# Four more chunks of q and k turned by a copy in DRAM and VectorE instead of by TensorE

## The chip, the cores and the metric

The kernel runs on one core of one Trainium2 chip. Five engines run their own instruction queues and meet at semaphores: TensorE (in the profile PE for matmuls, PEld for weight loads), VectorE (DVE), ScalarE (ACT), GpSimd (POOL) and SyncE (SP), which here does nothing but issue DMAs. A core has 16 DMA engines. The metric is the device time of one execution in microseconds; lower is better.

## The reference

Two blocks follow each other. The first is a linear attention with decay ("lightning attention"): batch 4, 8 heads, 768 positions, head dimension 64, in blocks of 64 positions.

```
for b in range(nb):                       # blocks of 64 positions
    intra = einsum(qb, kb) * Dmask        # lower triangular, lam ** distance
    out   = einsum(intra, vb) + einsum(qb * lam_pow, kv_state)
    kv_state = lam_block * kv_state + einsum(kb * rev_pow, vb)
```

The second takes the result as x, 3072 rows (batch times position) of 512, and runs four dense experts, each weighted by its share of the domain probabilities:

```
p = domain_probs / domain_probs.sum(-1)
for e in range(4):                        # w1[e]: 512 x 1024, w2[e]: 1024 x 512
    out += p[:, e:e+1] * (relu(x @ w1[e]) @ w2[e])
```

All is float32. The experts' products are the bulk of the arithmetic.

## The kernel before

**Tiling.** The 3072 rows are cut into three groups of 1024 (`NG` = 3), and each group with each of the four experts is a unit: 12 units, numbered 0 to 11 in the order of `units`. The products of a unit are made by Strassen's scheme with seven products, in most places nested twice, so that sums of blocks of the weights and of x are made by POOL, VectorE and through DRAM (`w1_ops`, `w2_ops`, `w2_sums`, `x_blocks`). While unit `at` makes its second product (line 1204, `w2t`), the first product of the next unit is made beside it (line 1145, weights in `ws_in`). Both go through seven products `i`, and each `i` through eight slots `x`. The order of all work is written out by this loop: slot number (`at` * 7 + `i`) * 8 + `x`. Outside of attention a product takes 12.95 us, so a slot is about 1.6 us. Unit 0 starts at 88.4 us of the trace, unit 1 at 191.4, unit 2 at 293.8. From unit 5 (`NEST`) on, other forms of the products take over.

**Attention** works on chunks of 128 positions of one batch: 6 chunks times 4 batches, n = 0 to 23, eight to a group. `where(n)` gives (chunk, batch). The first eight are made ahead of unit 0. The other 16 stand in the slots named by `AT`, from n = 8 on: slot `AT[n - 8]` is where `scores(n)` is issued, together with `values(n - 1)`. n = 8 to 15 are chunks 2 and 3, with (2,0), (2,1), (3,0), (3,1), (2,2), (2,3), (3,2), (3,3) in this order, n = 16 to 23 chunks 4 and 5 likewise. For each, `attention()` puts steps into the slots: `load_more(n)` (q and k), `load(n, "v")` seven slots ahead of the scores, `turn(n)`, and the scores.

**Turning.** Scores need q and k with the head dimension on the partitions. Two ways are there:

- By TensorE (`turn`, line 698): q and k are loaded as they lie (two DMAs each), eight transposes of 128x128 go to the PSUM banks s0 and s1, and ACT copies the two results to SBUF (lines 706 and 707). Before the change this is so for n = 0 to 15. Loads stand 7 slots ahead of the turn, and the turn 4 ahead of the scores; for n = 12 (`TURNED_FIRST`) these are 5 and 7.
- Across (`turn_across`, line 678), before the change for n = 16 to 23 (`comes_across`): DMAs from DRAM to DRAM first copy q and k into `across`, in stripes of 32 columns, so that 32 of the head dimension's columns of each head stand as rows of blocks of 32x32. `load_across` reads four blocks a head and partition (runs of 512 B), and VectorE transposes every 32x32 block of the 128x512 tile in place, one instruction for q and one for k. k is loaded once more as it lies, for the state's update (`decayed`, on POOL). Loads stand 5 slots ahead of the turn, and the turn 7 ahead of the scores.

**The copies** are 128 DMAs (`pieces`): for each batch 16 of q and then 16 of k, each of 32 columns of one head over chunks 4 and 5, in runs of 128 B, 256 runs in all. `trickle` issues the next one: one a step in the products that lead up to unit 0, one a slot in unit 0 (in odd slots from ACT's queue, else from SyncE's), and from unit 1 on one in every odd slot. Ahead of the loads of a chunk, `load_more` issues at once what is still missing of its batch.

**Order around the change.** SyncE issues its DMAs strictly in the program's order, and waits where one has to wait. On it stand, from slot to slot: the weights of the second product (`feed2`, three products ahead), those of the first (`feed`, in unit 1 in slots 0 and 1 of a product for the product after it), stores of sums made by POOL, the copies, and the loads of q, k and v. Work on VectorE that is not bound to a slot waits in the lists `lately` (attention) and `background` (operands of the experts) and is taken about one a slot, `lately` first. A planner's estimates (`busy`, `moved`, `asked`, `filled`) decide when POOL's chores begin.

Of the kernel before, what the change touches and what calls it, by code (L numbers as in the profile page):

```python
# [14 lines left out]
FP32 = mybir.dt.float32  # L15
# [6 lines left out]
def kernel(  # L22
# [32 lines left out]
    B, H, S, D = q.shape  # L55
    E, DM, F = moe_w1.shape
    NTOK, DOUT = out.shape
    P = nc.NUM_PARTITIONS
    C = P
    BL = C // 2  # L60
    NHP = H // 2
    NCH = S // C
    CPG = 8
    G = CPG * C
    NG = NTOK // G
# [14 lines left out]
    dram = ctx.enter_context(tc.tile_pool(name="sums", bufs=1, space=DRAM))  # L80
# [11 lines left out]
    def small(name):  # L92
        return pool.tile([P, W], FP32, name=name, tag="t")
# [7 lines left out]
    def packet(ap):  # L101
        n, step = 1, 1
        for stride, size in reversed(ap.ap[1:]):
            if stride != step or size == 1 and stride != 1:
                break
            n, step = n * size, step * size
        return n

    def send(out, in_, by=None):
        n = 4 * min(packet(out), packet(in_))  # L110
        moved[0] = max(moved[0], now[0]) + 4 * math.prod(out.shape) / n * (9 + n / 25) / 16 / 1714
        if by is None:
            asked[0] = max(asked[0], now[0]) + 0.27
        (by or nc.sync).dma_start(out=out, in_=in_)
# [35 lines left out]
    def where(n):  # L150
        g, x = divmod(n, CPG)
        return (x // 4, x % 4) if g == 0 else (2 * g + x // 2 % 2, 2 * (x // 4) + x % 2)
# [304 lines left out]

    SECOND = NCH - 2  # L460
    across = dram.tile([2, P, NHP, B, 8, 32], FP32, name="across")
    pieces = []

    def bring_across(b):
        for x, of in enumerate((q, k)):
            for y in range(4):
                for ac in range(NHP):
                    src = of[b, 4 * (y // 2) + ac, SECOND * C:, (y % 2) * 32:(y % 2 + 1) * 32]
                    to = across[x, y * 32:(y + 1) * 32, ac, b]
                    pieces.append((b, lambda by, to=to, src=src: send(  # L470
                        out=to, in_=src.rearrange("(t p) d -> p t d", p=32), by=by,
                    )))

    def trickle(m=1, by=None):
        for _ in range(m):
            if pieces:
                pieces.pop(0)[1](by)

    def comes_across(n):
        return where(n)[0] >= SECOND  # L480

    def load_across(n):
        c, b = where(n)
        for x, name in enumerate("qk"):
            t = small(f"{name}x")
            send(
                out=t[:].rearrange("p (h c) -> p h c", c=C),
                in_=across[x, :, :, b, (c - SECOND) * 4:(c - SECOND) * 4 + 4].rearrange("p h t d -> p h (t d)"),
            )
            nat[n, name + "x"] = t  # L490

    def load_more(n):
        if not comes_across(n):
            load(n, "qk")
        else:
            trickle(sum(b <= where(n)[1] for b, _ in pieces))
            load_across(n)
            load(n, "k")

# [38 lines left out]
    for r in range(2):  # L538
        for ac in range(NHP):
            h = 4 * r + ac  # L540
# [102 lines left out]
    def rest(n=1, force=False):  # L643
        for _ in range(n):
            take(background, force)
# [9 lines left out]
    def decayed(n):  # L655

        kn = nat[n, "k"]
        kd = kn if n >= CPG else small("kd")[:].rearrange("p (h d) -> p h d", d=D)
        nat[n, "kd"] = kd
        by = k_decay.rearrange("p r ac -> p ac r").unsqueeze(3).to_broadcast([P, NHP, 2, D])  # L660
        tt(nc.gpsimd, *(x.rearrange("p (ac r) d -> p ac r d", r=2) for x in (kd, kn)), by, ALU.mult)
# [194 lines left out]
        ))  # L856

    FILL = {1: 18, 2: 43}
    AT = (34, 40, 47, 53, 58, 94, 101, 108, 115, 147, 154, 167, 172, 203, 210, 223)
    TURNED_FIRST = CPG + 4  # L860
    steps = []

    def attention():

        first, last = CPG, NG * CPG - 1
        for n in range(first, last + 1):
            s = AT[n - first]
            turns_at = s - (7 if comes_across(n) or n == TURNED_FIRST else 4)

            def both(n=n):  # L870
                if n > first:
                    values(n - 1, ("s0", "s1"))
                scores(n, ("q02", "q12"))

            steps.append((turns_at - (5 if comes_across(n) or n == TURNED_FIRST else 7), lambda n=n: load_more(n)))
            steps.append((s - 7, lambda n=n: load(n, "v")))
            steps.append((turns_at, lambda n=n: turn(n, ("s0", "s1"))))
            if comes_across(n):
                steps.append((turns_at, lambda n=n: (decayed(n), nat.pop((n, "k")))))
            steps.append((s, both))  # L880
        steps.append((AT[last - first] + 5, lambda: values(last, ("s0", "s1"))))
        steps.append((AT[last - first] - 14, turn_gates))
        steps.sort(key=lambda s: s[0])
# [711 lines left out]
    def put_back():  # L1595
        n = len(copied)
        while copied:
            copied.pop(0)()
        return n
# [162 lines left out]
        lambda: own_weights("M1"), sum_own("S1", "A21", "A22", ALU.add), *w2_steps[0:4], mine["M1"], *w2_steps[4:],  # L1762
        raw["A12"],
    ))
    for b in range(B):
        bring_across(b)
    for m in SEQ0[2:]:
        if m == SEQ0[-1]:
# [42 lines left out]
    for at, (g, e) in enumerate(units):  # L1811
# [14 lines left out]
        for i in range(7):  # L1826
# [12 lines left out]
            if nested:  # L1839
                pair = (at * 7 + i) % 2 if ahead else i % 3  # L1840
                idle[:] = [(("q11", "q12"), ("q01", "q02"))[pair % 2], False]
                b = nested_product(at, SEQ3[i], (("q01", "q02"), ("q11", "q12"), ("g1", "g3"))[pair])
                if i < 6 and (at, SEQ3[i + 1]) != PLAIN:
                    inner_sums(at, SEQ3[i + 1])
            else:
                b = second_product(g, e, SEQ2[i], banks)
# [21 lines left out]
            for x, part in enumerate(order):  # L1868
                for f in part:
                    if f:  # L1870
                        f()
                now[0] += 1
                put = False
                if at == 0:
                    idle[:] = [("s0", "s1"), i < 3]
                    put = put_back()
                    take(own_sums)
                if nested and ahead:
                    idle[1] = x in (1, 4) and (at - 2 * E + 1, i, x) not in held_at
                    put = put_back()  # L1880
                added = first_steps.pop((at - 2 * E + 1, i, x), None)
                if added:
                    added()
                all_added(now[0])
                if joins and not background:
                    joined()
                elif added and x > 2 or put:
                    pass
                elif (ahead or x % 2 == 0 and x + i) and not (nests and i == 6 and x == 7):
                    if nested or nests:  # L1890
                        if lately:
                            take(lately)
                        else:
                            rest()
                        if at == 2 * E and i in (2, 3) and fits():
                            rest()
                    else:
                        took = False
                        for of in (lately, background, own_sums):
                            if of and (not took or fits() or of is background and len(of) > 4):  # L1900
                                take(of)
                                if of is lately and i == 0:
                                    take(of)
                                took = True
                if nested or nests:
                    take(aside)
                    if own_sums and (nested or fits()):
                        take(own_sums)
                if ending and fits():
                    end_first()  # L1910
                if nested and ahead and x in (1, 3) and fill3:
                    feed3(*fill3.pop(0))
                if turned_back and x > 0:
                    for y in turned_back.pop(0):
                        if SEQ3[i] == END[1]:
                            give(*y[:2], ("s0", "s1"), *y[2:])
                        else:
                            give_across(*y)
                if fill and at * 7 + i >= 6 and x in ((0, 1) if at * 7 + i < 13 else (1, 3, 5) if at * 7 + i == 13 else FEED[nested]):
                    feed(*fill.pop(0))  # L1920
                while steps and (at * 7 + i) * 8 + x == steps[0][0]:
                    steps.pop(0)[1]()
                if at == 0 or x % 2:
                    trickle(1, nc.scalar if at == 0 and x % 2 else None)
                for h in range(1, NG):
                    if x == 3 and 0 <= at * 7 + i - FILL[h] < 7:
                        x_fill(h, SEQ[at * 7 + i - FILL[h]])
                pump(PACE[g])
# [30 lines left out]
```

## Time and profile before

| | |
|---|---|
| median of 3 executions | 1144.79 us (1144.61 to 1146.84) |
| the profiled execution | 1146.52 us |
| its span, first to last instruction | 1144.7 us |
| TensorE busy (matmuls) | 1135.0 us, 99% of the span |
| VectorE, ACT, POOL busy | 765.6, 384.1, 766.5 us |
| moved by DMA | 269.22 MB, mean 235 GB/s |
| chain that ended last | PE 95%, POOL 2%, DVE 1%, issue 1% |

The page's first part gives busy times; its second cuts the span into 40 slices (28.6 us each) with a digit for the busy share in tenths, 9 being 90% or more. A group's line gives the source line, the engine, the operation, what is written from what is read, shapes and count, then busy time and mean ns of one, then the engine's idle time before it and what ended it. In the order of time, a line gives start and length in us. Landing times of DMAs are from issue to the last byte's semaphore.

### The profile page before, as it was taken

How to read it: one execution, taken by the hardware profiler on the slowest of the kernel's cores; microseconds unless marked ns; L12 is line 12 of the kernel's file. 1: busy time of each engine (PE TensorE's matmuls, PEld its weight loads, DVE VectorE, ACT ScalarE, POOL GpSimd, SP SyncE). 2: the span in 40 equal slices, each digit the busy share in tenths (PEclk: the TensorE clock that was granted, in tenths of full speed). 3: DMA queues.
4: the chain of work that ended last, by engine and by line, in shares of the span. 5: the costliest groups of instructions: out<-in, count | busy, mean ns of one | idle time of the engine just before them, and what ended most of it. 6: DMA issues, size and time to landing. Idle time of an engine off the chain costs nothing.

```text
span 1144.7 us, 22214 instructions
## 1 busy us (share of the span) xinstructions
PE 1135.0 (99%) x8015; PEld 990.5 (87%) x8015; DVE 765.6 (67%) x1466; ACT 384.1 (34%) x776; POOL 766.5 (67%) x734
## 2 busy tenths in 40 slices
PE   9999999999999999999999999999999999999998
PEld 7788888888888888888888888888888888888887
DVE  5576676576577748837665566778757576776785
ACT  4325223213312321232343442444354442342332
POOL 2657148646852974853884997895995783873885
PEclk9999999999999999999999999999999999999999
DMA  9795788898999999977867658976678757657552
GB/s 201 166 276 174 196 222 248 271 301 231 307 315 298 296 314 290 309 271 241 250 207 255 197 182 286 331 247 210 204 252 262 230 158 195 202 163 210 173 193 74
DMA packets 309148, 269.22 MB, mean 235 GB/s; under 512 B 141424, under 2 KB 244016, under 8 KB 309040
## 3 DMA queue, kind: packets, MB, share of 16 engines
q1 hardware_dynamic: 291360, 262.66, 75.2%
q10 hardware_dynamic: 17648, 5.15, 2.1%
q8 instruction: 64, 1.05, 0.4%
q14 instruction: 44, 0.36, 0.1%
q0 software_dynamic: 32, 0.00, 0.0%
HBM read 194.83 MB, written 77.10 MB: 238 GB/s over the span
## 4 chain that ended last, share of the span: by engine, by line
PE 95%; POOL 2%; DVE 1%; issue 1%; DMA 0%; ACT 0%; DVEq 0%; POOLq 0%; ACTq 0%
PE pg L1145 39%; PE pq L1511 23%; PE q L1204 21%; PE pM L1653 2%; PE pc L1653 2%; PE op L795 1%; PE sp L732 1%; PE op L813 1%; PE sp L739 1%; POOL acc L117 1%; PE qp L698 1%; PE pM L1378 1%; PE kp L698 1%; PE pg L1511 1%; DVE m L117 0%
## 5 line engine op out<-in xcount | busy, mean ns | idle before, releaser
L1145 PE MATMUL pg<-xs,ws_in 128*128 128x256 f32 x1960 | 470.7, 380 | 0.5 <-DVE m L117 0.5
L1145 PEld LDWEIGHTS pg<-xs,ws_in 128*128 128x128 f32 x1960 | 370.5, 190 | 54.4 <-DVE m L117 4.0
L117 DVE TENSOR_TENSOR m<-pg,m 128x512 f32<-128x512 f32 x374 | 255.9, 686 | 97.0 <-PE pg L1145 84.6
L1204 PE MATMUL q<-w2t,m 128*128 128x256 f32 x1120 | 265.5, 380 | 0.0
L1204 PEld LDWEIGHTS q<-w2t,m 128*128 128x128 f32 x1120 | 211.7, 190 | 29.2 <-issue 0.3
L117 DVE TENSOR_TENSOR sums<-pq,sums 128x256 f32<-128x256 f32 x272 | 113.2, 421 | 90.4 <-PE pq L1511 78.4
L117 POOL TENSOR_TENSOR m<-m,decay 128x512 f32<-128x512 f32 x91 | 114.7, 1273 | 81.5 <-ACT m L1162 64.6
L1511 PE MATMUL pq<-acc,w2t 128*128 128x256 f32 x688 | 169.2, 379 | 0.0
L1511 PEld LDWEIGHTS pq<-acc,w2t 128*128 128x128 f32 x688 | 130.5, 190 | 18.0
L1162 ACT ACTIVATE m<-m 128x512 f32<-128x512 f32 x99 | 62.4, 630 | 195.4 <-DVE m L117 190.5
L1222 DVE SCALAR_TENSOR_TENSOR acc<-q,gate,acc 128x256 f32<-128x256 f32 x108 | 52.1, 482 | 79.2 <-PE q L1204 78.7
L117 DVE TENSOR_TENSOR m<-m,m 128x512 f32<-128x512 f32 x108 | 91.1, 843 | 6.5 <-ACT m L1128 6.5
L1158 ACT COPY m<-pg 128x512 f32<-128x512 f32 x88 | 51.6, 586 | 122.6 <-PE pg L1145 118.5
L117 POOL TENSOR_TENSOR acc<-hT,hT 128x512 f32<-128x512 f32 x56 | 70.4, 1273 | 22.3 <-DVE hT L117 12.1
L1122 ACT COPY pg<-m 128x512 f32<-128x512 f32 x77 | 45.4, 590 | 111.0 <-DVE m L117 103.9
L117 POOL TENSOR_TENSOR acc<-hT,acc 128x512 f32<-128x512 f32 x56 | 71.3, 1273 | 6.5 <-PE pq L1511 2.7
L1511 PE MATMUL pq<-hT,w2t 128*128 128x256 f32 x288 | 70.0, 379 | 0.0
L117 POOL TENSOR_TENSOR w2o<-w2b 128x512 f32<-128x512 f32 x26 | 34.9, 1364 | 44.9 <-DMA w2b<-in_moe_w_dram 27.4
L1511 PEld LDWEIGHTS pq<-hT,w2t 128*128 128x128 f32 x288 | 54.7, 190 | 7.4
L117 POOL TENSOR_TENSOR kn<-kn,decay 128x512 f32<-128x512 f32 x16 | 18.5, 1157 | 59.8 <-PE kp L698 35.5
L1511 PE MATMUL pq<-m,w2t 128*128 128x256 f32 x228 | 55.4, 379 | 0.0
L1126 ACT COPY m<-pg 128x512 f32<-128x512 f32 x44 | 25.8, 586 | 88.2 <-PE pg L1145 83.5
(157 smaller groups left out, 1463.6 us busy)
## 6 DMA issues: line engine op xcount, KB each, us to landing
w2t<-w_ops SPq DMA_DIRECT2D x129, 256.0 KB, 3.2
ws_in<-w_ops SPq DMA_DIRECT2D x40, 512.0 KB, 4.4
ws_in<-w_ops SPq DMA_DIRECT2D x60, 256.0 KB, 3.9
ws_in<-w_ops SPq DMA_DIRECT2D x40, 384.0 KB, 4.1
w2b<-in_moe_w_dram SPq DMA_DIRECT2D x56, 256.0 KB, 5.4
w_ops<-ops SPq DMA_DIRECT2D x28, 512.0 KB, 4.8
w2t<-w_sums SPq DMA_DIRECT2D x40, 256.0 KB, 4.3
w_sums<-w2o SPq DMA_DIRECT2D x16, 512.0 KB, 4.1
```

The costliest lines, as they stand in the source:

```text
L117: eng.tensor_tensor(out=o, in0=a, in1=b, op=op)
L698: nc.tensor.transpose(out=x[:, ac * C:(ac + 1) * C], in_=y[:, 2 * ac:2 * ac + 2].rearrange("p r d -> p (r d)"), identity=ident[:],)
L732: nc.tensor.matmul(out=sp[r][half[x], ac * BL:(ac + 1) * BL], lhsT=hc(kT)[half[r], ac, blk[x]], rhs=hc(qT)[half[r], ac, blk[x]], start=(ac ...
L1122: nc.scalar.copy(out=banks[tags[1]][:], in_=new["11"][:])
L1126: nc.scalar.copy(out=o[:], in_=p[:])
L1145: nc.tensor.matmul(out=p[:, j * 256:(j + 1) * 256], lhsT=ws[i][:, j * P:(j + 1) * P], rhs=xs[i], start=(fresh and j == 0), stop=True, skip ...
L1158: nc.scalar.copy(out=new[at][:], in_=p[:])
L1162: nc.scalar.activation(out=new[at][:], in_=new[at][:], func=AF.Relu)
L1204: nc.tensor.matmul(out=p[:, s * DH:(s + 1) * DH], lhsT=h[A_OF[m]][:, c * 256 + s * P:c * 256 + (s + 1) * P], rhs=fed2[g, e, m][uu][:, c], ...
L1222: nc.vector.scalar_tensor_tensor(out=o, in0=x, scalar=w, in1=o, op0=ALU.mult, op1=ALU.add)
L1511: nc.tensor.matmul(out=p[:, 0:256], lhsT=fed3[e, m, x // 2][:, x % 2, c * P:(c + 1) * P], rhs=b[B_OF[i]][:, c * 256:(c + 1) * 256], start= ...
L1653: nc.tensor.matmul(out=p[:, s * 256:(s + 1) * 256], lhsT=a[c][:, f:f + P], rhs=b[:, c, j * 256:(j + 1) * 256], start=(s == 0 and c == 0 an ...
```

## The change

- `comes_across(n)` is now n >= 12 (`FIRST_ACROSS` = `CPG` + 4), so that n = 12 to 15, chunks 2 and 3 of batches 2 and 3, go across as well. TensorE's 32 transposes and ACT's 8 copies for them go, 8 transposes on VectorE come.
- The tile `across` has 16 blocks of 32 positions in place of 8, from chunk 2 on. The copies of batches 2 and 3 take all four chunks 2 to 5 (512 runs of 128 B, 64 KB), those of batches 0 and 1 chunks 4 and 5 as before (256 runs, 32 KB). There are still 128 copies.
- Their order is by `rank`: batch 0 (short), 2 (long), 3 (long), 1 (short), where it was 0, 1, 2, 3.
- In unit 1 one more copy goes out in each product, in slot 4.
- Scores of n = 13 and 14 move from slots 94 and 101 to 91 and 99. With the loads 12 slots ahead of the scores, chunk n = 12 is loaded in slot 46 as before, n = 13 in slot 79 (before 83), n = 14 in 87 (before 90), n = 15 in 96 (before 97).
- `TURNED_FIRST` goes, since n = 12 has its distances by `comes_across`.

```diff
-    SECOND = NCH - 2
-    across = dram.tile([2, P, NHP, B, 8, 32], FP32, name="across")
+    FIRST_ACROSS = CPG + 4
+    across = dram.tile([2, P, NHP, B, 16, 32], FP32, name="across")
     pieces = []
+    rank = {0: 0, 2: 1, 3: 2, 1: 3}

     def bring_across(b):
+        c = min(where(n)[0] for n in range(FIRST_ACROSS, NG * CPG) if where(n)[1] == b)
         for x, of in enumerate((q, k)):
             for y in range(4):
                 for ac in range(NHP):
-                    src = of[b, 4 * (y // 2) + ac, SECOND * C:, (y % 2) * 32:(y % 2 + 1) * 32]
-                    to = across[x, y * 32:(y + 1) * 32, ac, b]
-                    pieces.append((b, lambda by, to=to, src=src: send(
+                    src = of[b, 4 * (y // 2) + ac, c * C:, (y % 2) * 32:(y % 2 + 1) * 32]
+                    to = across[x, y * 32:(y + 1) * 32, ac, b, (c - 2) * 4:]
+                    pieces.append((rank[b], lambda by, to=to, src=src: send(
                         out=to, in_=src.rearrange("(t p) d -> p t d", p=32), by=by,
                     )))
...
     def comes_across(n):
-        return where(n)[0] >= SECOND
+        return n >= FIRST_ACROSS
...
-                in_=across[x, :, :, b, (c - SECOND) * 4:(c - SECOND) * 4 + 4].rearrange("p h t d -> p h (t d)"),
+                in_=across[x, :, :, b, (c - 2) * 4:(c - 1) * 4].rearrange("p h t d -> p h (t d)"),
...
-            trickle(sum(b <= where(n)[1] for b, _ in pieces))
+            trickle(sum(x <= rank[where(n)[1]] for x, _ in pieces))
...
-    AT = (34, 40, 47, 53, 58, 94, 101, 108, 115, 147, 154, 167, 172, 203, 210, 223)
-    TURNED_FIRST = CPG + 4
+    AT = (34, 40, 47, 53, 58, 91, 99, 108, 115, 147, 154, 167, 172, 203, 210, 223)
...
-            turns_at = s - (7 if comes_across(n) or n == TURNED_FIRST else 4)
+            turns_at = s - (7 if comes_across(n) else 4)
...
-            steps.append((turns_at - (5 if comes_across(n) or n == TURNED_FIRST else 7), lambda n=n: load_more(n)))
+            steps.append((turns_at - (5 if comes_across(n) else 7), lambda n=n: load_more(n)))
...
-    for b in range(B):
+    for b in rank:
         bring_across(b)
...
-                if at == 0 or x % 2:
+                if at == 0 or x % 2 or at == 1 and x == 4:
                     trickle(1, nc.scalar if at == 0 and x % 2 else None)
```

## The prediction

> **What bounds the kernel now.** I read the page's first two parts, then stretches of the time in which the four chunks are loaded, then the groups by line, then TensorE's and SyncE's instructions in order of time there. From the page:
>
> ```profile
> span 1144.7 us, 22214 instructions
> PE 1135.0 (99%) x8015; PEld 990.5 (87%) x8015; DVE 765.6 (67%) x1466; ACT 384.1 (34%) x776; POOL 766.5 (67%) x734
> ...
> PEclk9999999999999999999999999999999999999999
> DMA  9795788898999999977867658976678757657552
> ```
>
> TensorE is the bound, at full clock, and nothing but its work counts. The view of stretches (engines' busy time, then clock, share of the 16 DMA engines, GB/s) shows the next resource behind it:
>
> ```profile
> 88.40:191.40 103.00, 103.00 (x910) 90.52 (x909) 70.25 (x143) 33.22 (x68) 57.23 (x61) 1.00 0.73 200
> 191.40:219.70 28.30, 28.30 (x249) 24.57 (x248) 12.81 (x31) 8.34 (x17) 21.81 (x27) 1.00 0.80 260
> 219.70:261.70 42.00, 42.00 (x318) 36.93 (x318) 29.63 (x48) 7.06 (x15) 18.39 (x19) 1.00 0.99 304
> ```
>
> TensorE has no idle time in any of them, and from 219.7 to 261.7 us the DMA engines have none either (0.99). The groups by line give what is removed and what replaces it (busy, mean of one):
>
> ```profile
> L698 PE MATMUL qp<-ident,qn 128*128 128x128 f32 x64 | 10.5, 288 | 0.0
> L698 PE MATMUL kp<-ident,kn 128*128 128x128 f32 x64 | 10.1, 283 | 0.1
> L706 ACT COPY qT<-qp 128x512 f32<-128x512 f32 x16 | 9.4, 590 | 31.5 <-PE qp L698 31.5
> L678 DVE STREAM_TRANSPOSE qx<-qx 128x512 f32<-128x512 f32 x8 | 5.6, 698 | 0.0
> ```
>
> TensorE's instructions in order of time around chunk 13's turn:
>
> ```profile
> 249.08 1.89 PE L1204 MATMUL q<-w2t,m 128*128 128x256 f32 x8
> 250.81 0.60 PE L698 MATMUL qp<-ident,qn 128*128 128x128 f32 x4
> 251.24 0.60 PE L698 MATMUL kp<-ident,kn 128*128 128x128 f32 x4
> 251.68 1.89 PE L1145 MATMUL pg<-xs,ws_in 128*128 128x256 f32 x8
> ```
>
> The transposes start at 250.81 and the next product at 251.68: a turn holds TensorE 0.87 us. SyncE's queue in order of time (start, time to issue), around the loads of chunks 13 and 14:
>
> ```profile
> 231.65 0.57 SPq L114 DMA_DIRECT2D across<-in_k_dram  x1
> ...
> 233.38 0.42 SPq L114 DMA_DIRECT2D ws_in<-w_ops  x1
> ...
> 237.83 1.09 SPq L174 DMA_DIRECT2D qn<-in_q_dram  x2
> ...
> 248.36 0.46 SPq L114 DMA_DIRECT2D ws_in<-w_ops  x1
> ...
> 252.29 0.42 SPq L114 DMA_DIRECT2D ws_in<-w_ops  x1
> ...
> 257.14 4.52 SPq L174 DMA_DIRECT2D kn<-in_k_dram  x2
> ```
>
> Call the three ws_in feeds X, Y and Z: X and Y bring the first parts of the weights for products 4 and 5 of unit 1, Z the second part for product 5. They landed 5.7, 6.0 and 10.1 us after issue, so at 239.1, 254.4 and 262.4. TensorE's first matmuls with them started at 247.35, 263.40 and 268.6. Margins: 8.2, 9.0 and 6.2 us. That 10.1, and two kn issues of 4.52 us, show a queue that is already full.
>
> **The change, part by part.**
>
> Removed from TensorE: 4 chunks x 8 transposes, 4 x 0.87 = **3.5 us**. TensorE has no idle time from 88 us on beyond a few tenths here and there, so without a new wait all of it comes off the end (a 0.6 us wait for POOL and VectorE at 741.8 could take some back).
>
> Removed from ACT: 8 copies of 0.59 us; added on DVE: 8 transposes of 0.70 us, 5.6 us in all. DVE is busy 70.25 of 103.00, 12.81 of 28.30 and 29.63 of 42.00 us in the stretches concerned, which hides them; without that cover they cost 5.6 us. Among the eight chunks that already go this way, one whose transpose stands a slot ahead of its scores made TensorE wait for nothing. POOL's k decay no longer waits for the transposes (5.3 us idle at 251.9); POOL is not the end of the chain there, so zero.
>
> Issues: 128 copies before and after, and 4 loads a chunk before and after (two q, two k; then one q, one k across, two k natural). In unit 1 the copies go out five a product in place of four: 0.6 us of SyncE each, in the price of the queue below. The planner counts more traffic and starts some POOL chores a slot later; POOL is 67% busy, so zero. Without that cover, the tightest feed of unit 1, which waits for POOL's sums (landed 217.4, used 221.5), has 4.1 us to spare for a slot of 1.6 us, so still zero.
>
> DMA work: the trace's packets of 128, 256 and 512 B took 13, 19 and 28 ns. A copy of 256 packets is 256 x 13 / 16 = 0.21 us of all engines, a long one 0.42. A chunk's q and k are 4 x 512 x 19 / 16 = 2.4 us natural, and 2 x 512 x 28 / 16 + 1.2 = 3.0 us across. In all 64 x 0.21 + 4 x 0.6 = 15.8 us. Up to 191 us the share of 0.73 takes it. From 216 to 262 us (share 0.98) it can't all be taken.
>
> The Trainium skill ("DMA: Bandwidth & Descriptors", Specifications) gives about 27 GiB/s an engine as line rate and 512 B as the least transfer that reaches it; at line rate a long copy would be an estimated 0.14 us, and the sum below would end at about -1.8 us. The trace's 13 ns for 128 B is a third of that rate, as the page warns, and decides.
>
> Where it lands: counting the slots, 23 copies go out ahead of unit 0, 56 in it and 14 up to slot 79, where chunk 13 is now loaded (load 12 slots ahead of scores at 91). It needs 96, so 3 long ones go out at once there, about 232.3 to 233.5 us, and the kx load right behind them has to wait until they land. The copies nearest to it landed 3.7 to 4.6 us after issue, so SyncE is held from about 234.8 to 238, 3.2 us, with X, Y, Z and everything else queued behind. I take 2 us of that as lost to the DMA engines, since qx (0.9 us) and a backlog still feed them; bounds 0 and 3.2.
>
> Queue work newly ahead of Z since 216 us: copies, 12 long and 6 short in place of 12 short, 3.7 us; chunk 13, 0.6; chunk 14, whose load moves from slot 90 (behind Z) to 87 (ahead of Y), 3.0. Sum 7.3, plus 2.0 held, less 0.7 for the room in a share of 0.98: 8.6 us. Z's margin is 6.2, less two turns that TensorE no longer makes by then (1.75): 4.5. Z is late by **4.1 us**. X has 3.5 + 3.0 (all of chunk 13 comes ahead of it) + 2.0 - 0.7 = 7.8 against 8.2 - 0.9: late by 0.5, within Z's 4.1, since a stall at X moves Z's due time as well. Y has 8.6 against 7.2: 1.4, likewise within. Later feeds have margins of 7.7 and 10.6, with dips in the DMA share at 262, 276 and 282 us, so the queue recovers and nothing is added. Bounds: with nothing held and 3 us of room found in the dips the queue's 4.3 us stays inside 4.5, no stall; with 3.2 held and no room, 10.5 - 4.5 = 6.0, and 2 more if chunk 13's scores, three slots earlier, wait for v, 8.0.
>
> Sum: -3.5 + 4.1 = **+0.6 us**, bounds -3.5 and +4.5. The profiled execution took 1146.5 us (span 1144.7), 1.7 above the median of 1144.8; on the median the sum gives 1145.4.
>
> **The rivals.** A change under 0.2% (2.3 us) can hardly be told from none. *The forecast:* the stalls eat the gain, total between 1.2 and 5.8 us; 1145.4, within 1142.5 to 1147.1.
>
> *The queue takes it.* No feed is late and 3.5 us come off: 1141.3. For it: margins of 6 to 9 us, no wait of TensorE on a feed in all of unit 1, dips in GB/s (68 in one slice near 250 us) that show spare engine time, an order in which SyncE's delay costs the DMA engines nothing. Against: the share of 0.99, and Z's 10.1 us.
>
> *SyncE's hold decides the other way.* Its place is slot 79: kx of chunk 13 waits for the last three long copies, and behind it stand X, Y, Z and v of chunk 13. If the three land as slowly as the copy issued at 234.8 (7.4 us), SyncE is held 6.1 us, 2.9 more than above, X is late by 3.4 and Z by 7.0: -3.5 + 7.0 = +3.5, 1148.3. It decides for slower from a total stall of 5.8 us on. For it: SyncE waits in order (the trace has it waiting 10.9 us for POOL's sums, with feeds behind). The Trainium skill ("DMA: Bandwidth & Descriptors", Anatomy of one DMA) says DMA engines don't wait on semaphores, the issuing sequencer does; were it otherwise there would be no hold, and the sum -1.4 us. Against it: the full queue empties meanwhile, and later landings are quicker.
>
> **How the numbers follow.** Chances: forecast 0.37; queue takes it 0.32 (faster); hold decides 0.31 (slower). The range from 1141.0 (no stall, with run-to-run 0.3) to 1149.5 leaves out some 0.1; the forecast's own range is 1142.5 to 1147.1.
>
> **What would show it.** Right: 96 transposes on line 698 in place of 128, 24 stream transposes of qx and kx on DVE; an idle time of SyncE of 3 us or more ahead of kx near 235 us, with the copies as releaser; X, Y or Z landing at or after TensorE's first matmul with them, and 1 to 6 us of idle TensorE between 245 and 272 us, none elsewhere. Wrong: TensorE busy without a gap in that stretch (then -3.5), stalls for feeds in unit 0 or unit 2, or a DVE wait at the moved chunks' scores.

## The result, and the profile after

The changed kernel took **1159.21 us** (median of 5 runs, 1158.10 to 1161.58); the kernel before took 1145.41 beside it (5 runs, 1144.61 to 1146.84). The ratio is 1.0126, with a 95% interval of 1.0114 to 1.0138: slower by 1.3%, and outside the forecast's range.

The page of the changed kernel, most of the lines that were shown of before, and the chain:

```profile
span 1157.4 us, 22150 instructions
PE 1135.9 (98%) x7983; PEld 990.0 (86%) x7983; DVE 771.1 (67%) x1474; ACT 380.1 (33%) x768; POOL 764.1 (66%) x734
...
DMA  8796898989889999878658778976668866657552
...
PE 89%; DMA 4%; POOL 2%; SPq 2%; issue 1%; DVE 1%; ACT 0%; POOLq 0%; DVEq 0%; ACTq 0%
```

TensorE's busy time did not fall (1135.9 us against 1135.0), though it has 32 instructions fewer: from 15.5 to 18.9 and from 776.7 to 783.5 us it runs at half clock, which the kernel before does only in its last microsecond. The span is 12.7 us longer. DMA and SyncE's queue now hold 6% of the chain that ended last. The last of the forecast's three stretches (engines' busy time with counts, clock, DMA share, GB/s):

```profile
219.70:261.70 42.00, 38.53 (x297) 33.55 (x296) 32.66 (x53) 5.40 (x12) 19.70 (x17) 1.00 0.89 263
```

It lost 3.5 us of TensorE, where it had lost nothing. The groups show the edit as described: 96 transposes on TensorE and 24 on VectorE, half of each for q (shown) and half for k.

```profile
L680 DVE STREAM_TRANSPOSE qx<-qx 128x512 f32<-128x512 f32 x12 | 8.4, 700 | 0.1
...
L700 PE MATMUL qp<-ident,qn 128*128 128x128 f32 x48 | 8.2, 298 | 0.0
```

What TensorE waited for from 88 us on (total, times, longest), the four largest entries. Before, this list held one entry, 0.5 us for VectorE, which is here too:

```profile
PE pq L1512 <- DMA w2t<-w_ops: 6.5, 1, 6.5
PE pg L1146 <- DMA ws_in<-w_ops: 3.7, 2, 3.5
PE sp L734 <- issue: 2.2, 2, 1.1
PE sp L741 <- DMA vn<-in_v_dram: 0.6, 1, 0.6
...
```

The second entry is X (3.47 us, at 249.54) and Y (0.25 us). The first was in none of the forecast's cases: it lies in unit 7, over 400 us behind the last copy. Matching the same matmul in both traces, the changed kernel is 1.4 us ahead when unit 1 begins, 1.6 behind at 300 us, 3.5 behind from 420 to 740 us, and 12.7 behind from 800 us to the end. So there are two losses: **about 5 us in units 1 and 2 (net of the transposes that go there), and 9.2 us at 770 to 790 us**. The lead of 1.4 us is not all gain: 0.8 of it stands already when unit 0 begins, ahead of the first transpose that goes.

**The first loss.** SyncE's queue from the copies of slot 79 to X (start, time to issue):

```profile
231.28 5.41 SPq L114 DMA_DIRECT2D across<-in_k_dram  x6
236.73 0.63 SPq L114 DMA_DIRECT2D qx<-across  x1
238.99 0.56 SPq L114 DMA_DIRECT2D kx<-across  x1
239.60 1.16 SPq L174 DMA_DIRECT2D kn<-in_k_dram  x2
240.81 0.62 SPq L114 DMA_DIRECT2D across<-in_q_dram  x1
241.47 1.11 SPq L114 DMA_DIRECT2D w2b<-in_moe_w_dram  x2
242.62 0.94 SPq L114 DMA_DIRECT2D w2t<-w_sums  x2
243.61 0.43 SPq L114 DMA_DIRECT2D ws_in<-w_ops  x1
```

X goes out at 243.61; before, at 233.38. It lands 5.8 us after its issue, much as before (5.7). The 10.2 us are SyncE's own: eight more DMAs stand ahead of X (four copies, qx, kx, two kn), each 0.5 to 1.2 us to issue, SyncE stands idle for 1.6 us ahead of kx and 0.8 us within the copies, the queue was already 2.0 us late at the w2b loads ahead of them, and 0.1 us is left for slower issues.

**The second loss.** TensorE's instructions in order of time, then the stretch behind the stop:

```profile
778.51 2.04 PE L1512 MATMUL pq<-m,w2t 128*128 128x256 f32 x4 [6.50 <-DMA w2t<-w_ops]
780.34 1.91 PE L1512 MATMUL pq<-acc,w2t 128*128 128x256 f32 x4
782.05 2.61 PE L1146 MATMUL pg<-xs,ws_in 128*128 128x256 f32 x8
784.50 1.89 PE L1512 MATMUL pq<-acc,w2t 128*128 128x256 f32 x8
```

```profile
778.40:786.00 7.60, 7.49 (x23) 6.23 (x24) 2.47 (x5) 1.89 (x4) 1.68 (x2) 0.66 1.02 354
```

After a stop of 6.5 us four matmuls take 1.9 to 2.0 us, as long as eight do from 784.50 on: the granted clock of that stretch is 0.66 in the mean. The stop costs 6.5 us and the half clock behind it some 2.5. What the w2t feeds waited for stands in SyncE's queue:

```profile
754.40 0.56 SPq L114 DMA_DIRECT2D ws_in<-w_ops  x1
755.06 0.38 SPq L114 DMA_DIRECT2D w_ops<-w2o  x1
...
763.25 0.37 SPq L114 DMA_DIRECT2D w_ops<-w2o  x1
766.66 0.32 SPq L114 DMA_DIRECT2D w_ops<-ops  x1
...
769.90 0.44 SPq L114 DMA_DIRECT2D w_ops<-ops  x1
770.44 1.96 SPq L114 DMA_DIRECT2D w2b<-in_moe_w_dram  x4
772.50 1.36 SPq L114 DMA_DIRECT2D w2t<-w_ops  x3
```

From 755.06 to 769.90 SyncE issues 18 stores of `w_ops`, three chores' worth (two that came late and a forced one), waits 3.0 us for POOL's sum ahead of 766.66, then loads the next expert's blocks, and only at 772.50 comes to the w2t feeds. Before, six w2t feeds went out in the 18 us behind the same ws_in feed (then at 750.87), each when a buffer came free:

```profile
753.52 4.95 SPq L114 DMA_DIRECT2D w2t<-w_ops  x3
...
761.60 0.32 SPq L114 DMA_DIRECT2D w2t<-w_ops  x1
...
765.92 4.63 SPq L114 DMA_DIRECT2D w2t<-w_ops  x3
```

Why three chores stand there follows from the program: it decides when a chore begins while it writes out the order, from its own numbers (a chore waits while `moved`, the traffic counted so far, reaches `FULL` = 4 slots ahead). Slots in which four of POOL's chores begin:

```
                                             before  changed  count alone  copies earlier
pause in w1 of expert 3 (`moved` 3.7 / 5.9)     90       94        94            91
pause in w1 of expert 0                        190      204       200           190
first `ready` of w2 operands, expert 3         253      288       288           253
last `ready` of w2 operands, expert 0          371  391 forced  391 forced       371
```

(The table is worked out from the program. The third and fourth columns are two of the experiments below, the fourth the one with its own count.) Three long copies, qx and kx at slot 79, and chunk 14's loads at slot 87, put the count at 5.9 in slot 90, where it was 3.7. Four slots late, the chores meet the loads of chunks 21 and 22 and lose ten more; that carries them past slot 264, and from 264 to 287 no chore may begin (`resting`). At slot 391 `feed3` asks for expert 0's operands, finds the last of them missing and forces what is left, and one chore behind it (`until`).

### The profile page after: what moved, and what is told of

It is laid out like the page before. It is cut to its first block, busy times and chain, and to the rows that moved or that the text cites. A ratio compares the mean times of both kernels' runs of the same rounds, so it can differ in the third digit from the quotient of the medians.

```text
span 1157.4 us, 22150 instructions
## 1 busy us (share of the span) xinstructions
PE 1135.9 (98%) x7983; PEld 990.0 (86%) x7983; DVE 771.1 (67%) x1474; ACT 380.1 (33%) x768; POOL 764.1 (66%) x734
## 4 chain that ended last, share of the span: by engine, by line
PE 89%; DMA 4%; POOL 2%; SPq 2%; issue 1%; DVE 1%; ACT 0%; POOLq 0%; DVEq 0%; ACTq 0%
PE pg L1146 38%; PE pq L1512 23%; PE q L1205 19%; PE pc L1654 2%; SPq L114 2%; PE pM L1654 1%; DMA w2b<-in_moe_w_dram 1%; PE op L797 1%; DMA ws_in<-w_ops 1%; PE sp L734 1%; PE sp L741 1%; PE op L815 1%; POOL acc L117 1%; DMA vn<-in_v_dram 1%; POOL ops L117 1%
```

## The experiments

Medians of runs beside the kernel before on the same chip, and the ratio to it with its 95% interval. The ratio is formed from all the runs, so it can differ a little from the quotient of the two medians:

| kernel | us | before, us | ratio |
|---|---|---|---|
| the changed kernel | 1159.21 | 1145.41 | 1.0126 (1.0114 to 1.0138) |
| count neutral | 1155.15 | 1146.28 | 1.0073 (1.0041 to 1.0105) |
| count alone, on the kernel before | 1152.62 | 1146.28 | 1.0052 (1.0035 to 1.0069) |
| count neutral, chunk 13 loaded later | 1159.94 | 1146.28 | 1.0104 (1.0071 to 1.0138) |
| count neutral, copies earlier | 1148.15 | 1146.02 | 1.0025 (1.0007 to 1.0042) |
| own count, copies earlier | 1148.89 | 1145.90 | 1.0018 (1.0003 to 1.0033) |
| that, scores of 13 and 14 back | 1146.70 | 1146.13 | 1.0000 (0.9988 to 1.0012) |
| transposes off TensorE, no copies | 1143.49 | 1146.02 | 0.9988 (0.9972 to 1.0004) |
| copies alone | 1149.63 | 1146.02 | 1.0035 (1.0020 to 1.0051) |
| three chunks, copies earlier | 1145.69 | 1146.02 | 1.0000 (0.9986 to 1.0014) |
| four chunks, copies in unit 0 | 1147.90 | 1145.90 | 1.0013 (1.0001 to 1.0025) |
| three chunks, copies in unit 0 | 1147.63 | 1145.90 | 1.0016 (1.0004 to 1.0028) |
| batch 2 alone | 1146.45 | 1146.13 | 1.0005 (0.9993 to 1.0016) |

My theory after the result: the late loss comes of the planner's count alone, and X was late by its place in SyncE's queue. The rivals: the traffic itself makes the late loss; X is late because the 16 DMA engines are full.

### Count neutral

```diff
-    def send(out, in_, by=None):
+    def send(out, in_, by=None, share=1):
...
-        moved[0] = max(moved[0], now[0]) + 4 * math.prod(out.shape) / n * (9 + n / 25) / 16 / 1714
-        if by is None:
+        moved[0] = max(moved[0], now[0]) + share * 4 * math.prod(out.shape) / n * (9 + n / 25) / 16 / 1714
+        if by is None and share:
...
-                        out=to, in_=src.rearrange("(t p) d -> p t d", p=32), by=by,
+                        out=to, in_=src.rearrange("(t p) d -> p t d", p=32), by=by, share=0.5 if rank[b] in (1, 2) else 1,
...
+                share=0 if n < 2 * CPG else 1,
```

> The changed kernel, but the planner counts a long copy as a short one and the loads of chunks 12 to 15 from `across` at nothing, as it did before; every DMA stays. Theory (the counts alone hold POOL's chores back, until a run of them is forced at slot 391 and holds SyncE's queue ahead of the w2t feeds): the stop of 6.5 us at 778 us and the half-clock matmuls behind it go, 9.2 us, so 1159.2 - 9.2 = 1150.0 us; the stop of 3.5 us at product 4 of unit 1 stays. Rival (the late loss comes of the traffic itself, or of the products' being 3.5 us later against the queue): the stop at 778 us stays and the time is 1159 us.

Measured 1155.15 (1151.21 to 1161.19). The stop at 778 us is gone: the trace is 8.55 us behind the kernel before at 420 us and still 8.55 at 800. But units 1 and 2 lost more than in the changed kernel's trace: the stop at X is 3.81 us and is now followed by half clock (eight matmuls take 2.61 us, the next eight 2.98, where 1.89 is usual), and v of a later chunk is 2.1 us late, again with half clock behind it. SyncE's queue shows a second hold that I had not thought of, at chunk 17's load:

```profile
341.26 0.56 SPq L114 DMA_DIRECT2D across<-in_k_dram  x1
...
342.51 0.58 SPq L114 DMA_DIRECT2D qx<-across  x1
346.63 0.57 SPq L114 DMA_DIRECT2D kx<-across  x1
```

Batch 1's copies now go last, and the last of them goes out right ahead of chunk 17's load. It landed 5.3 us after issue, at 346.6, and kx went out at 346.63, with SyncE idle for 3.5 us. The late loss is gone as the theory had it; 1150.0 was missed. The count is neutral to within a slot or two only: by the program, chores behind slot 90 begin mostly one to two slots earlier than before, and from slot 288 on in the slots of before.

### Count alone, on the kernel before

```diff
-                    pieces.append((b, lambda by, to=to, src=src: send(
-                        out=to, in_=src.rearrange("(t p) d -> p t d", p=32), by=by,
+                        ..., share=2 if b >= 2 else 1,
...
         if not comes_across(n):
             load(n, "qk")
+            if n >= CPG + 4:
+                moved[0] = max(moved[0], now[0]) + 2 * 512 * (9 + 512 / 25) / 16 / 1714
+                asked[0] = max(asked[0], now[0]) + 0.54
```

> The kernel before, with its own copies and its transposes on TensorE, but the planner counts as if batches 2 and 3 had long copies and chunks 12 to 15 were loaded across. Not a byte more is moved. Theory (counts alone make the late loss): no stop in unit 1, a run of forced chores at the end of unit 6 and a stop of some 6.5 us for w2t<-w_ops near 780 us with half-clock matmuls behind it: 1145.4 + 9.2 = 1154.6 us. Rival (traffic or a later base): 1145.4 us.

Measured 1152.62 (1151.63 to 1153.21): +0.52% (0.35 to 0.69), some 6 us, with the same transfers and transposes as before, in another order. No stop in unit 1; the one large stop is this:

```profile
772.83 1.98 PE L1514 MATMUL pq<-m,w2t 128*128 128x256 f32 x4 [4.36 <-DMA w2t<-w_ops]
```

The clock of the 4.2 us behind it is 0.59. The rival falls. The stop is 4.4 us, not 6.5, and why it is shorter than in the changed kernel was not separated.

### Chunk 13 loaded later

```diff
-            steps.append((turns_at - (5 if comes_across(n) else 7), lambda n=n: load_more(n)))
+            steps.append((turns_at - {13: 3}.get(n, 5 if comes_across(n) else 7), lambda n=n: load_more(n)))
```

> As the kernel with the neutral count, and chunk 13's loads two slots later, in slot 81 in place of 79, so that both of product 4's ws_in feeds (X among them) go out ahead of the copies and the loads. Theory (X was late by its place in SyncE's queue, not by what the DMA engines could move): X lands some 8 us earlier, its stop of 3.5 us goes, no other stop takes its place: 1150.0 - 3.5 = 1146.5 us. Rival (the 16 DMA engines were full and the work only moves): product 5's feeds (Y, Z) or chunk 13's scores stop TensorE for 2 to 3.5 us instead: 1148.5 to 1150 us.

Measured 1159.94: both missed. X went out at 236.92 and landed 3 us ahead of its use, but the loads moved and the turn did not. SyncE's hold at kx was now 4.2 us, and VectorE, which works in order too, stood at chunk 13's transposes with a product's eviction behind them (start, length, idle before):

```profile
247.00 0.71 DVE L681 STREAM_TRANSPOSE qx<-qx 128x512 f32<-128x512 f32 x1 [7.46 <-DMA qx<-across]
...
249.78 0.71 DVE L681 STREAM_TRANSPOSE kx<-kx 128x512 f32<-128x512 f32 x1 [1.70 <-DMA kx<-across]
250.42 0.65 DVE L117 TENSOR_TENSOR m<-pg,m 128x512 f32<-128x512 f32 x1
```

TensorE stopped for 7.13 us at 251.12, waiting for that eviction. So the run can't price X's stop; it shows what a late copy costs on the other side.

### Copies earlier, with neutral and with full count

```diff
-                    trickle(1, nc.scalar if at == 0 and x % 2 else None)
+                    trickle(2 if at == 0 and x == 5 else 1, nc.scalar if at == 0 and x % 2 else None)
```

> As the kernel with the neutral count, and in unit 0 slot 5 of each product issues two copies in place of one (from ACT's queue), seven more in all, so that the copies which chunk 13 needs are all out some 5 slots (8 us) ahead of its load, and chunk 17's likewise. No byte is added. Theory (SyncE is held at a kx load that stands right behind the last copies it needs; that hold, not the bandwidth, makes X and the v of chunk 18 late): SyncE no longer waits ahead of kx near 235 and 346 us, X is late by less than 1 us, the half-clock stretch behind its stop goes too; against the neutral count's profile that is -3.8 - 2.9 - 2.1: about 1147 us. Rival (DMA engines full in unit 1): X is as late as before, 1152 to 1155 us.

Measured 1148.15 (1142.96 to 1152.66, 10 runs). SyncE's wait ahead of kx is 0.1 us, X goes out at 240.57, three us earlier, and lands 5.4 us after that (5.8 in the changed kernel), 0.4 us ahead of its use. So SyncE's time ahead of X made it late, the hold and the issues of the missing copies, and not a slower landing; 1148.15 lies near the theory's 1147 and clear of the rival's 1152. What is left is Z, the second part for product 5, as the forecast had named it:

```profile
268.53 1.10 PE L1147 MATMUL pg<-xs,ws_in 128*128 128x256 f32 x4 [2.15 <-DMA ws_in<-w_ops]
```

The same line alone, put into the changed kernel with its full count:

> The changed kernel with its own, full counts, and in unit 0 slot 5 of each product issues two copies in place of one, as in the run with earlier copies. Worked out with the planner's own numbers, POOL's chores then begin at most one slot later than before and from slot 141 on in the slots of before, since three copies no longer go out at once at slot 79. Theory (both large losses, SyncE's hold at kx and the late burst of chores, hang on those copies that were still missing): no stop at 778 us, no stop at X; 1148 us like the run with earlier copies and neutral counts, 11 us under the changed kernel. Rival (the counts or the traffic hurt by themselves, whatever the slot): the stop at w2t<-w_ops near 770 us stays, 1152 us or more.

Measured 1148.89 (1145.87 to 1150.91, 12 runs), as the theory had it: some 11 us of the 14 hung on the three copies that were still missing at slot 79, and go when seven copies are issued earlier, though no byte is saved. In unit 7 the chores are where they were, and TensorE is busy throughout:

```profile
765.00:780.00 15.00, 15.00 (x71) 13.22 (x70) 11.51 (x24) 7.76 (x15) 8.90 (x10) 1.00 0.70 223
```

At Z 1.52 us are left, and 1.3 us at chunk 14's scores.

### Scores of 13 and 14 back

```diff
-    AT = (34, 40, 47, 53, 58, 91, 99, 108, 115, 147, 154, 167, 172, 203, 210, 223)
+    AT = (34, 40, 47, 53, 58, 94, 101, 108, 115, 147, 154, 167, 172, 203, 210, 223)
```

> The changed kernel with its own counts and the earlier copies, and scores of chunks 13 and 14 back in slots 94 and 101, as before: chunk 13 is loaded in slot 82 and 14 in slot 89, behind both feeds of products 4 and 5 (X, Y, Z), and their turns move by the same slots, so VectorE doesn't wait for the loads. Four chunks go across. Theory (order in SyncE's queue: the loads ahead of X and Z make these late): the stop at Z of 1.5 to 2.2 us goes: 1146.5 us or less, at best 1146.0 - 3.5 = 1142.5. Rival (the bytes, not the order): a stop of 1.5 us or more in unit 1 all the same, at another feed, at v or at the scores: 1148 to 1149 us.

Measured 1146.70 (1142.75 to 1149.15, 12 runs), ratio 1.0000. The stop at Z fell from 1.52 to 0.51 us, so order accounts for most of it. The kernel now equals the one before but is not faster: in its trace it is 3.8 us ahead at 300 us and 0.2 behind at 420, by a stop of 1.69 us at chunk 16's scores in unit 2, half clock behind it, and smaller ones. Of the 3.8 us, 2.4 stand already when unit 0 begins, where the work is the same: single traces of these kernels differ by up to 4 us there (2.4 ahead here, 1.7 behind in the run with earlier copies and full count), so a lead or lag in one trace is read from unit 0 on.

### The parts alone

Transposes off TensorE, without copies (chunks 12 to 15 of the kernel before):

```diff
+        if CPG + 4 <= n < 2 * CPG:
+            decayed(n)
+            ...
+            soon(n, *(lambda x=x, y=y: blocks_only(x, y) for x, y in ((qT, qn), (kT, kn))))
+            return
         qp = bank(tags[0], "qp")
```

> The kernel before, with the 32 transposes of chunks 12 to 15 off TensorE and eight block-wise transposes on VectorE of the q and k as they were loaded; no copy in DRAM is longer and nothing more is loaded. It leaves out the change of order that the copies make, so these chunks' scores are computed from wrongly ordered blocks. It measures the gain by itself. Theory (3.5 us, as in the forecast): 1146.3 - 3.5 = 1142.8 us. Rival (waits elsewhere take the gain back, or VectorE's eight transposes delay the products' evictions): 1145 to 1146.5 us.

Measured 1143.49 (1141.66 to 1150.49, 10 runs), 2.5 us under the median before; the interval of the ratio runs from -0.28% to +0.04%, so the runs don't exclude that nothing is gained. In its trace the same matmuls are 1.4 us ahead of the kernel before at unit 0, where nothing has gone yet, and 4.1 ahead at 300 us: 2.7 us for the four turns, of which 0.9 is lost again behind. It shows no wait of TensorE over 0.5 us; the larger of the two entries from 88 us on:

```profile
PE pg L1158 <- DVE m L117: 0.9, 3, 0.5
```

Copies alone (`AT` and `TURNED_FIRST` as before, long copies and their order kept, neutral count):

```diff
-        return n >= FIRST_ACROSS
+        return n >= 2 * CPG
```

> The change's copies in DRAM alone: long copies for batches 2 and 3, their order 0, 2, 3, 1 and the extra one a product in unit 1, counted by the planner as before; but chunks 12 to 15 are loaded and turned on TensorE as before, in the slots of before, and nobody reads the added half of the copies. It measures the traffic without the loads that wait for it. Theory (the traffic alone is taken by the queue; only a load right behind its copies hurts): no stop at X, Y or Z over 0.5 us; chunk 17's load still stands right behind batch 1's last copies, which now go last, so a hold of SyncE near 345 us and up to 2 us there: 1146.3 to 1148.5 us. Rival (the 16 DMA engines are full and the added 12.8 us of their work stop TensorE): X, Y or Z late by 3 us or more: 1149 us and above.

Measured 1149.63 (1146.06 to 1153.46, 10 runs): +0.35% (0.20 to 0.51). The theory's upper end is missed; the rival's time is met, but not at its place. No ws_in feed is late; the natural q of chunk 14 is, in the profiled execution (which, at 1153.1, was among the longest):

```profile
268.98 0.63 PE L701 MATMUL qp<-ident,qn 128*128 128x128 f32 x4 [3.88 <-DMA qn<-in_q_dram]
```

It went out at 259.83 (before 253.49) and took 8.6 us to land (9.3). So the copies hurt by themselves, and again by making SyncE late, not by slower landings: five copies a product in place of four, in a stretch where two issues can take 3.2 us (kn at 244.91). The longer copies and the one more a product were not separated.

### Other mixes

Three chunks, on the kernel with neutral count and earlier copies (`AT` as before):

```diff
-        return n >= FIRST_ACROSS
+        return n >= FIRST_ACROSS and n != 13
```

> As the kernel with earlier copies, but chunk 13 is turned on TensorE and scores of 13 and 14 stand in slots 94 and 101 as before: three chunks go across. Theory (chunk 13's loads ahead of X, at slot 79, are what crowds SyncE's queue most): no stop in unit 1 over 0.5 us, gain 3 x 0.87 = 2.6 us: 1146.3 - 2.6 = 1143.7 us. Rival (what is left of the traffic still stops TensorE in units 1 and 2, 2 us or more): 1146 to 1148 us.

Measured 1145.69, ratio 1.0000: no gain, between the theory and the rival, with stops at feeds of 1.1 us at 220 and 1.0 us at 299 us.

The copies moved to unit 0, with four chunks and with three (these with the edit above as well):

```diff
-                if at == 0 or x % 2 or at == 1 and x == 4:
-                    trickle(1, nc.scalar if at == 0 and x % 2 else None)
+                if at == 0 or x % 2:
+                    trickle(2 if at == 0 and i < 4 - (x % 2 == 0) else 1, nc.scalar if at == 0 and x % 2 else None)
```

> As the kernel with the neutral count, but 28 copies more go out in unit 0 (two a slot in the odd slots of its first four products and the even slots of its first three), and the extra one a product in unit 1 goes: unit 1 has 21 short copies left, all before slot 98, unit 2 none. Theory (what is left after earlier copies, the stop of 2.2 us at Z and 1.6 us at chunk 14's scores, is the copies' share of a full queue in unit 1): no stop over 0.5 us in unit 1; 1146.0 - 3.5 = 1142.5 to 1143.5 us. Rival (unit 0, at a share of 0.74 to 0.93, can't take 12 us more either): feeds late in unit 0, or chunks 9 to 11's loads late, 1146 to 1150 us.

> As the kernel with the copies in unit 0, but chunk 13 is turned on TensorE and scores of 13 and 14 stand in slots 94 and 101 as before: three chunks across. Theory: 0.87 us less gain than with four, and no stop: 1146.0 - 2.6 = 1143.4 us. If the four chunks' loads still crowd the queue ahead of X and Z, this one is the faster of the two by 1 to 3 us.

Measured 1147.90 and 1147.63, both in the first one's rival's range: the traces of both stop for 2.37 us at 104 to 105 us in unit 0, on POOL's `ops`, a stop that no other run has. With four chunks Z is still 2.06 us late. The two times are 0.3 us apart, so here the fourth chunk doesn't cost the 1 to 3 us that were thought possible.

Half of the change (neutral count, `AT` as before):

```diff
-    rank = {0: 0, 2: 1, 3: 2, 1: 3}
+    rank = {0: 0, 2: 1, 1: 2, 3: 3}
...
-        return n >= FIRST_ACROSS
+        return n >= 2 * CPG or n in (12, 14)
...
-                if at == 0 or x % 2 or at == 1 and x == 4:
+                if at == 0 or x % 2:
```

> Half of the change: batch 2's chunks 12 and 14 alone go across (32 long copies in place of 64, order 0, 2, 1, 3, no extra copy in unit 1, slots and POOL's chores as before); 13 and 15 stay on TensorE. Theory (a smaller part of the traffic fits the queue's margins of 6 to 9 us): no stop over 0.5 us, gain 2 x 0.87 = 1.75 us: 1146.0 - 1.75 = 1144.3 us. Rival (any of it costs as much as it gains): 1145.5 to 1147.5 us.

Measured 1146.45: the rival's range. Half the traffic costs about what half the transposes give, at v of a later chunk (0.9 us) and elsewhere. No kernel of these beats the one before.

## Why the prediction was wrong

**The step that failed** is "The planner counts more traffic and starts some POOL chores a slot later; POOL is 67% busy, so zero". The slot later was right for slots 74 to 88. I asked what one slot would cost unit 1's tightest feed and went no further, where the delay grew to 4, 14 and 35 slots and ended in forced chores. That costs 0.52%, about 6 us, in the run with the count alone, and 9.2 us in the changed kernel's trace. The busy share of POOL says nothing here: the stop is at SyncE, which waits in order for POOL's sum. It was not the only term: with the neutral count, and so without this loss, the kernel still took 8.9 us more than before, so the terms below would have missed the range too. By medians, 6.3 us for the count alone and 8.9 for the rest make 15.2, against 13.8 measured for both.

**The gain**, 3.5 us by the forecast: 2.5 us between medians (by the interval, from 0.5 lost to 3.2 gained), and 2.7 us in one trace from unit 0 to 300 us. By that trace the mechanism is right and 3.5 a little too much; the medians alone can't tell the gain from none. ACT and VectorE hid their part, but for a wait of 0.2 us for VectorE near 184 us that the kernel before doesn't have, and except where chunk 13 was loaded later.

**SyncE's hold** was forecast at 3.2 us and was 1.6 us in the changed kernel's trace. The mechanism is right, and the harm of the three copies larger: with seven copies more in unit 0, some 11 us go. That harm came also by two ways that the forecast lacked, the count of three copies at once and the same hold at chunk 17's load (1.0 us in the changed kernel's trace, 3.5 with the neutral count). The Trainium skill ("DMA: Bandwidth & Descriptors", Anatomy of one DMA) says the issuing sequencer waits on the semaphore, not the DMA engine; the traces agree: kx went out within 0.2 us of the landing of the last copy, in five holds of three kernels.

**X** was forecast 0.5 us late and was 3.5 late. The failed term is the queue's: I added the DMA engines' time for the work ahead of X (7.8 us), where X moved by SyncE's own time, 10.2 us: eight issues, 5.7 us, idle time 2.4, and a queue 2.0 us late already. The rival "SyncE's hold decides the other way" had X late by 3.4 us and 1148.3 in all; its stop was there, made otherwise, and that the two sizes agree is luck.

**Y and Z**: Y 0.25 us late; Z on time in the changed kernel, probably since the stop at X gave it time: with that stop gone, Z is late by 2.15 and 1.52 us, where 4.1 was forecast.

**"None elsewhere"** was wrong as well: TensorE stood 1.0 and 1.1 us within the scores of chunks 14 and 16, and 0.6 us for a v, none of which the sum had.

## What to carry to other kernels

Where a program lays out its own order from counted costs, an edit that changes a count changes the order everywhere behind it: compare the order of the whole program, and look for places where late work is forced or may not begin. A load right behind the last write that it needs turns the write's latency into a hold of the whole in-order queue; put some microseconds of other work between them, on the engine that reads it too. On a queue near its limit, price an added transfer by the issuing engine's time as well as by the DMA engines'.

## What was not expected of the hardware

**A stop costs more than itself.** Stops of 6.50, 4.36, 3.88 and 3.81 us were followed by a granted clock of 0.59 to 0.66 over some 4 to 7.6 us; after the 3.47 us at X in the changed kernel it stayed at 1.00, after 1.69 us (scores back) it was 0.70, and of two stops of 2.37 us (copies in unit 0) one was followed by 0.58, one by 1.00.

Cut finer, the clock in these traces is 1.00 or 0.50 with nothing between, and every half that follows a stop lasts 3.41 us or twice that. So the time can be laid out in steps of 3.41 us, counted in each trace from where the clock changes. First the step ahead of a half and the half itself in the run with scores back, then the two steps across which the stop at X falls in the changed kernel, and the next (the length of the step and TensorE's busy time come first, the clock is the third figure from the end):

```profile
298.32:301.73 3.41, 1.72 (x55) 1.46 (x48) 1.32 (x3) 1.11 (x5) 2.75 (x4) 1.00 0.85 258
301.73:305.15 3.42, 3.42 (x9) 2.72 (x9) 0.96 (x3) 0.00 (x0) 3.19 (x6) 0.50 1.05 349
```

```profile
244.19:247.60 3.41, 1.88 (x9) 1.32 (x7) 2.23 (x4) 1.12 (x2) 2.38 (x2) 1.00 0.82 230
247.60:251.02 3.42, 1.48 (x7) 1.36 (x8) 1.04 (x2) 0.00 (x0) 2.42 (x4) 1.00 1.03 405
251.02:254.43 3.41, 3.41 (x18) 3.00 (x17) 3.24 (x5) 0.00 (x0) 3.41 (x3) 1.00 1.19 328
```

What counts, over all steps at full clock behind 88 us in the fourteen traces, is how long TensorE was busy within one step: eight with at most 1.29 us were all followed by half clock, none with at least 1.78 us was, and of the three between, 1.50 and 1.72 us were (with 64x64 matmuls among them) and 1.48 us, at X, was not. That is why stops of one length differ: one of the two of 2.37 us lies within one step (1.04 us busy), the other across two (at least 1.89). The Trainium skill ("TensorE: Matmul & The Clock Gate", Part 1: The HAM clock gate) gives half rate after an idle window of about 3.4 us that runs free of the kernel. The length of the steps agrees, and that they run free of the stops; but in these traces a step need not be idle from end to end. A step at half clock costs up to 1.7 us of TensorE's work (3.41 / 2). That may be why runs of one kernel spread so (1151 to 1161 us with neutral count); it was not tried.

**Waits that the profile calls "issue"** stood within groups of 64x64 matmuls, 1.0 to 1.7 us each, in the kernel before (41.3 and 46.4 us) as in others. In all six that were followed up, in four traces, a single packet of the instruction queue (16 KB) began 2.3 to 2.7 us before TensorE went on: between 270.50 and 270.75 for 273.19 in the changed kernel, between 38.75 and 39.00 for 41.33 in the kernel before. The likely reading is that TensorE, in a run of short matmuls, waits for its next instructions behind a full DMA queue. This is argued from the times; no run separated it.
